# Attention matmuls in four 64x64 tiles, with background matmuls in clumps and tanhs held back, in a fused conformer block

## The chip, the cores and the metric

One core of one Trainium2 chip runs the kernel. The metric is the device time of one execution in microseconds (us), the median of several. Executions of one kernel mostly agree within 1%; a run more than 1.5% above the fastest of the same kernel is called slow and is left out of ratios.

The engines that matter: here PE does matmuls (its weight loads are listed apart, as PEld; in the changed kernel those of O start 0.02 us after matmuls of S that take 0.40 us), ACT does exp and tanh, DVE does elementwise work and copies out of PSUM. In the traces below each engine works through its instructions in program order and stands in front of one whose inputs are not ready (ACT for 0.48 us in before, in front of a tanh, with the next exp's input ready). "Granted clock" is the TensorE clock as the profile gives it: 1.0 or 0.5 in every stretch of before.

## The reference, cut to what matters

```python
B, T, D, H = 2, 4000, 144, 4                 # Dh = 36
x = x + 0.5 * (silu(layernorm(x) @ w_ff1a) @ w_ff1b)
q, k, v = heads(layernorm(x) @ w_qkv)
x = x + (softmax(q @ k.T * Dh**-0.5) @ v) @ w_o      # full attention over 4000 keys
h = layernorm(x) @ w_pw1
h = h[..., :D] * sigmoid(h[..., D:])
x = x + silu(depthwise_conv5(h)) @ w_pw2
x = x + 0.5 * (silu(layernorm(x) @ w_ff2a) @ w_ff2b)
return layernorm(x)
```

## The kernel before

Attention runs in 32 groups (batch, chunk of 500 queries, pair of heads) of 32 iterations (125 keys each), 1024 in all. One iteration is: S, scores of two heads into two PSUM banks; exp of both banks by ACT into PT; O, PT times V into one bank that accumulates over a group. A column of ones in V gives the softmax sum. Everything else (layer norms, feed-forward, convolution) is cut into small steps of Python generators, called background (bg) here. `Pump.slot` emits up to two such steps after each iteration, within a budget per engine. Sigmoid and silu are made of tanh, so bg needs ACT too.

```python
def emit_S(n):                       # two matmuls, K = 64 rows each (row tiles), M = 125
    for hh in range(2):
        op("pe", "matmul", PSV[0:TB, 2 * (n % 2) + hh, 0:CH], lhsT=KT[64 * hh:64 * hh + 64, p, k0:k0 + TB],
           rhs=QT[64 * hh:64 * hh + 64, p, q0:q0 + CH], ...)

def emit_O(n):                       # two matmuls, K = 125 rows, M = 64 (column tiles)
    for hh in range(2):
        op("pe", "matmul", PSV[64 * hh:64 * hh + 64, 4 + gi % 2, 0:CH], lhsT=VA[0:TB, blk, 2 * p + hh, :],
           rhs=PT[0:TB, n % NPT, hh, :], start=kt == 0, stop=kt == NKT - 1, ...)

def tanh_gate(bk, rows):             # emitted at once, so in front of the next exp
    t = yield from thp.take()
    op("act", "activation", TH[0:rows, t, :], PSV[0:rows, bk, 0:CH], ACT.Tanh, ...)
    return t

def epilogue(banks, b, qc, p, og):   # once per group
    op("dve", "tensor_copy", OTF[:, og % 2, :], PSV[:, 4 + og % 2, 0:CH], ...)
    yield
    bk = yield from banks.take()
    for i in range(NB):
        op("pe", "transpose", PSV[0:TB, bk, i * 128:(i + 1) * 128], OTF[:, og % 2, i * TB:(i + 1) * TB], IDF[:, :], ...)
    yield
    # ... normalise, output projection ...

emit_S(0)
for n in range(len(its)):
    if n + 1 < len(its):
        emit_S(n + 1)
    emit_exp(n)
    if n > 0:
        emit_O(n - 1)
        # ... last one of a group: pump.add(epilogue(...), first=True)
    pump.slot()                      # up to two bg steps, banks 6 and 7
```

The softmax here doesn't subtract the row's maximum and nothing guards it: scores larger than these inputs give would overflow.

Of the kernel before, what the change touches and what calls it, by code (L numbers as in the profile page):

```python
# [5 lines left out]
ACT = mybir.ActivationFunctionType  # L6
ALU = mybir.AluOpType
BF16 = mybir.dt.bfloat16
F32 = mybir.dt.float32
# [4 lines left out]
HD = 72  # L14
FF = 576
KCONV = 5
TB = 125
NB = 4
CH = 500
# [8 lines left out]
class Rec:  # L28
# [13 lines left out]
    def op(self, eng, name, *a, r=(), w=(), q=None, cost=0.0, **k):  # L42
        o = Op()
        o.eng, o.name, o.a, o.k, o.q = eng, name, a, k, q
        o.deps, o.inc, o.cnt = [], False, 0
        lane = eng if q is None else "q:" + q
        o.idx = self.n.get(lane, 0)
        self.n[lane] = o.idx + 1
        for key in r:
            h = self.hist.setdefault(key, ([], []))  # L50
            o.deps += [(d, True) for d in h[0]]
            h[1].append(o)
        for key in w:
            h = self.hist.setdefault(key, ([], []))
            o.deps += [(d, False) for d in h[0] + h[1] if d is not o]
            if h[1] and not (len(h[1]) == 1 and h[1][0] is o):
                self.hist[key] = ([o], [])
            else:
                h[0].append(o)
        self.ops.append(o)  # L60
        self.cost[eng] += cost
        return o
# [82 lines left out]
def bass_standalone__conformer_family_zipformer__speech_kernel(  # L145
# [17 lines left out]
    CPB = T // CH  # L163
    NBLK = N // TB
    NKT = T // TB

    R = Rec(nc)
    op = R.op

    def sb(name, shape, dt=BF16):  # L170
        return nc.alloc_sbuf_tensor(name, [128] + list(shape), dt)
# [9 lines left out]
    TH = sb("TH", [NTH, CH])  # L181
    HT = sb("HT", [NHT, 5, CH])
    QT = sb("QT", [2, N])
    KT = sb("KT", [2, N])
    VA = sb("VA", [NBLK, H, 64])
    NPT = 3
    PT = sb("PT", [NPT, 2, CH])
    OTF = sb("OTF", [2, CH], F32)
    RD = sb("RD", [2, NB, 2], F32)
    U = sb("U", [2, T + 4])  # L190
# [18 lines left out]
    PSV = PS[:, :].rearrange("p (b n) -> p b n", n=512)  # L209
# [138 lines left out]
            banks.give(bk)  # L348
        yield

    def tanh_gate(bk, rows):
        t = yield from thp.take()
        op("act", "activation", TH[0:rows, t, :], PSV[0:rows, bk, 0:CH], ACT.Tanh, bias=0.0, scale=0.5,
           r=[("ps", bk)], w=[("TH", t)], cost=0.47)
        return t

    def ff(banks, c, s, WA, WB, nm, silu):
        h = yield from htp.take()
# [71 lines left out]
    def post1(banks, c):  # L430
        b, cc = c // CPB, c % CPB
        s = yield from ln_tr(banks, c)
        for hf in range(2):
            bk = yield from banks.take()
            for k in range(2):
                op("pe", "matmul", PSV[0:HD, bk, 0:CH], lhsT=WP1[0:HD, k, D + hf * HD:D + (hf + 1) * HD],
                   rhs=XT[0:HD, s, k, :], start=k == 0, stop=k == 1, r=[("XT", s), "WP1"], w=[("ps", bk)], cost=0.21)
            t = yield from tanh_gate(bk, HD)
            banks.give(bk)
            bk = yield from banks.take()  # L440
            for k in range(2):
                op("pe", "matmul", PSV[0:HD, bk, 0:CH], lhsT=WP1[0:HD, k, hf * HD:(hf + 1) * HD],
                   rhs=XT[0:HD, s, k, :], start=k == 0, stop=k == 1, r=[("XT", s), "WP1"], w=[("ps", bk)], cost=0.21)
            yield
            op("dve", "scalar_tensor_tensor",
               out=U[0:HD, hf, 2 + cc * CH:2 + (cc + 1) * CH].rearrange("p (n i) -> p i n", i=NB),
               in0=TH[0:HD, t, :].rearrange("p (i n) -> p i n", i=NB), scalar=1.0,
               in1=PSV[0:HD, bk, 0:CH].rearrange("p (i n) -> p i n", i=NB), op0=ALU.add, op1=ALU.mult,
               r=[("TH", t), ("ps", bk), "U0"], w=[("U", cc)], cost=0.6)
            banks.give(bk)  # L450
            thp.give(t)
        xtp.give(s)
        yield
# [31 lines left out]

    def epilogue(banks, b, qc, p, og):
        c = b * CPB + qc
        op("dve", "tensor_copy", OTF[:, og % 2, :], PSV[:, 4 + og % 2, 0:CH], r=[("ps", 4 + og % 2)],
           w=[("OTF", og % 2)], cost=0.6)
        yield  # L490
        bk = yield from banks.take()
        for i in range(NB):
            op("pe", "transpose", PSV[0:TB, bk, i * 128:(i + 1) * 128], OTF[:, og % 2, i * TB:(i + 1) * TB],
               IDF[:, :], r=[("OTF", og % 2), "IDF"], w=[("ps", bk)], cost=0.2)
        yield
        v = PSV[0:TB, bk, :].rearrange("p (i h d) -> p i h d", i=NB, h=2)
        op("dve", "reciprocal", RD[0:TB, og % 2, :, :], v[:, :, :, DH], r=[("ps", bk)], w=[("RD", og % 2)],
           cost=0.15)
        if p == 0:
            an_slot[qc % 2] = yield from anp.take()  # L500
        a = an_slot[qc % 2]
        op("dve", "tensor_tensor",
           AN[0:TB, a, :, p * HD:(p + 1) * HD].rearrange("p i (h d) -> p i h d", h=2), v[:, :, :, 0:DH],
           RD[0:TB, og % 2, :, :].rearrange("p i (h o) -> p i h o", o=1).to_broadcast([TB, NB, 2, DH]),
           op=ALU.mult, r=[("ps", bk), ("RD", og % 2)], w=[("AN", a)], cost=0.37)
        banks.give(bk)
        yield
        if p == 1:
            s = yield from tr(banks, AN[0:TB, a, :, :], ("AN", a), lambda: anp.give(a))
            yield from residual(  # L510
                banks, c, lambda i: [(XT[0:HD, s, k, i * TB:(i + 1) * TB], WO[0:HD, k, :]) for k in range(2)], 1.0,
                [("XT", s), "WO"], 0.06)
            xtp.give(s)
            att_done.add(c)
# [37 lines left out]
    def drain(threads, width):  # L552
        live = []
        threads = list(threads)
        while threads or live:
            while threads and len(live) < width:
                live.append(threads.pop(0))
            for t in list(live):
                try:
                    next(t)  # L560
                except StopIteration:
                    live.remove(t)
# [7 lines left out]
    drain([pre(all_banks, 0, True), first()] + [pre(all_banks, c, True) for c in range(1, CPB)], 4)  # L570

    bg = Banks([6, 7])
    pump = Pump({"pe": 0.35, "dve": 0.75, "act": 0.25})

    def pre_thread(cs):
        for c in cs:
# [2 lines left out]
    def post1_thread(b):  # L579
        for c in range(b * CPB, (b + 1) * CPB):  # L580
            while c not in att_done or (b and min(c - CPB + 1, CPB - 1) not in conv_done):
                yield
            yield from post1(bg, c)
            u_done.add(c)

    def post2_thread(b):
        for c in range(b * CPB, (b + 1) * CPB):
            while c not in u_done or (c + 1 < (b + 1) * CPB and c + 1 not in u_done):
                yield
            yield from post2(bg, c)  # L590
# [4 lines left out]
    def emit_S(n):  # L595
        gi, kt = its[n]
        b, qc, p = groups[gi]
        k0 = b * T + kt * TB
        q0 = b * T + qc * CH
        kc, qcc = b * CPB + kt // NB, b * CPB + qc  # L600
        for hh in range(2):
            op("pe", "matmul", PSV[0:TB, 2 * (n % 2) + hh, 0:CH], lhsT=KT[64 * hh:64 * hh + 64, p, k0:k0 + TB],
               rhs=QT[64 * hh:64 * hh + 64, p, q0:q0 + CH], start=True, stop=True,
               r=[("WKT", kc), ("WQT", qcc)], w=[("ps", 2 * (n % 2) + hh)])

    def emit_exp(n):
        s = 2 * (n % 2)
# [3 lines left out]
    def emit_O(n):  # L611
        gi, kt = its[n]
        b, qc, p = groups[gi]
        blk = b * NKT + kt
        for hh in range(2):
            op("pe", "matmul", PSV[64 * hh:64 * hh + 64, 4 + gi % 2, 0:CH], lhsT=VA[0:TB, blk, 2 * p + hh, :],
               rhs=PT[0:TB, n % NPT, hh, :], start=kt == 0, stop=kt == NKT - 1, skip_group_check=True,
               r=[("PT", n % NPT), ("VA", blk // NB)], w=[("ps", 4 + gi % 2)])

    pump.add(pre_thread(range(CPB, NCH)))  # L620
    pump.add(post1_thread(0))
    pump.add(post2_thread(0))
    emit_S(0)
    for n in range(len(its)):
        if n + 1 < len(its):
            emit_S(n + 1)
        emit_exp(n)
        if n > 0:
            emit_O(n - 1)
            if its[n - 1][1] == NKT - 1:  # L630
                gi = its[n - 1][0]
                pump.add(epilogue(bg, *groups[gi], gi), first=True)
                if gi == CPB * 2 - 1:
                    pump.add(post1_thread(1))
                    pump.add(post2_thread(1))
        pump.slot()
    emit_O(len(its) - 1)
    gi = len(groups) - 1
    for i in (0, 1, 2, 3):
        bg.give(i)  # L640
    drain([epilogue(bg, *groups[gi], gi)] + pump.threads, 8)

    R.finish(group_qs=("w0", "w1", "w2"))
    with nc.Block() as block:
# [29 lines left out]
```

## Time and profile before

| | before |
|---|---|
| time, median of the runs at hand before the change | 1429.57 us (1429.03 to 1439.14) |
| first exp to last exp (the stage) | 1229 us |
| ahead of it / after it | 133.5 / 67 us |
| clock 0.5 within the stage | 247 us |

The page of the kernel before: busy shares in 40 slices (each digit a tenth; PEclk is the granted clock), the chain of work that ended last, and four groups of instructions (output<-inputs, shapes, count, busy us, mean ns, idle us just before and what ended it).

```profile
PE   4888899899889989888889988888888888888855
ACT  2032987787887876888976888998989898989821
PEclk9655988888998975899986999999999899989965
...
PE 51%; ACT 39%; DVE 6%; issue 1%; POOL 1%; DMA 1%; ACTq 0%; POOLq 0%; DVEq 0%
...
L121 ACT ACTIVATE PT<-PS 125x1000 bf16<-125x1000 f32 x1024 | 960.3, 1021 | 110.9 <-PE PS L121 105.2
L121 PE MATMUL PS<-QT,KT 64*125 64x500 bf16 x2048 | 469.0, 455 | 124.2 <-ACT PT L121 78.2
L121 PE MATMUL PS<-PT,VA 125*64 125x500 bf16 x2048 | 440.8, 427 | 0.6 <-ACT PT L121 0.5
...
L121 ACT ACTIVATE TH<-PS 128x500 bf16<-128x500 f32 (+1 forms) x184 | 107.9, 586 | 148.6 <-PE PS L121 148.6
```

PE and ACT share the chain, and neither is full. ACT stood idle for 148.6 us in front of tanhs that waited for PE.

One bg iteration in the timeline of before (start us, duration us, engine, instruction, count; in brackets the idle time before it and what ended it):

```profile
615.76 1.89 ACT L121 ACTIVATE PT<-PS 125x1000 bf16<-125x1000 f32 x2
...
616.81 0.42 PE L121 MATMUL PS<-QT,KT 64*125 64x500 bf16 x2 [0.72 <-ACT PT L121]
...
617.17 0.11 PEld L121 LDWEIGHTS PS<-PT,VA 125*64 125x64 bf16 x2 [0.22 <-issue]
617.17 0.40 PE L121 MATMUL PS<-PT,VA 125*64 125x500 bf16 x2
...
617.50 0.60 PE L121 MATMUL PS<-XT,WA 72*128 72x500 bf16 x2
...
618.03 0.42 PE L121 MATMUL PS<-QT,KT 64*125 64x500 bf16 x2
618.14 0.59 ACT L121 ACTIVATE TH<-PS 128x500 bf16<-128x500 f32 x1 [0.48 <-PE PS L121]
...
618.62 1.00 ACT L121 ACTIVATE PT<-PS 125x1000 bf16<-125x1000 f32 x1
```

Read it from the ACT lines. The exps end at 617.65. S for the next exp was computed at 616.81 and has been ready for long, but the tanh stands in front of that exp, and the tanh needs the WA matmuls, which PE reaches only after S and O. ACT idles 0.48 us. The steps on PE are 0.36 us (S to O) and 0.33 us (O to bg), though matmuls of 500 columns and one shape follow each other after 0.21 to 0.22 us (medians in before at full clock: 0.212 for the convolution, 0.221 for WA). Below, 0.21 us is taken for 500 columns.

For the whole stage, take the distance from each exp to the next, subtract 0.888 us (the pace of exps in a row) and 0.464 us for each tanh in between, and sum: 242 us are lost in before, 105 of them in intervals at clock 0.5.

### The profile page before, as it was taken

To read this page: it belongs to the slowest core of one execution; us is meant where nothing else is said; L and a number is where in the kernel's file an instruction comes from. 1 tells how busy PE (TensorE), PEld (TensorE's weight loads), DVE (VectorE), ACT (ScalarE), POOL (GpSimd) and SP (SyncE) were. 2 spreads that over 40 slices of the span, in tenths; PEclk is the share of its full clock that TensorE was granted. 3 is DMA by queue.
4 is the path that set the end of the run, shared out by engine and by line. 5 is a ranking of instruction groups with operands and counts; after the bars stand their busy time and mean duration, and the time that the engine had idled before them with its cause. 6 is when DMAs were issued, how large, how long until landed. Compare 5 with 4: busy or idle time off the path is not lost.

```text
span 1429.6 us, 16367 instructions
## 1 busy us (share of the span) xinstructions
PE 1225.1 (86%) x6626; PEld 492.8 (34%) x6626; DVE 527.3 (37%) x1564; ACT 1073.5 (75%) x1250; POOL 109.3 (8%) x173
## 2 busy tenths in 40 slices
PE   4888899899889989888889988888888888888855
PEld 2544333333333333332332333233333333333322
DVE  5756434344443423233332334032323232323234
ACT  2032987787887876888976888998989898989821
POOL 3120000000100000000100001000000000000001
PEclk9655988888998975899986999999999899989965
DMA  3000000000000000000000000000000000000000
GB/s 91 1 1 1 1 0 0 1 0 0 1 1 1 1 5 1 5 2 4 5 2 3 5 4 3 3 1 5 1 5 1 4 1 5 0 5 1 4 0 8
DMA packets 6397, 6.60 MB, mean 5 GB/s; under 512 B 1746, under 2 KB 6322, under 8 KB 6322
## 3 DMA queue, kind: packets, MB, share of 16 engines
q1 hardware_dynamic: 4160, 4.61, 1.0%
q10 hardware_dynamic: 2162, 0.96, 0.3%
q8 instruction: 51, 0.84, 0.2%
q14 instruction: 24, 0.20, 0.0%
HBM read 3.26 MB, written 2.30 MB: 4 GB/s over the span
## 4 chain that ended last, share of the span: by engine, by line
PE 51%; ACT 39%; DVE 6%; issue 1%; POOL 1%; DMA 1%; ACTq 0%; POOLq 0%; DVEq 0%
PE PS L121 51%; ACT PT L121 33%; ACT TH L121 6%; POOL RS L121 1%; DVE ST L121 1%; DVE XN L121 1%; DVE OTF L121 1%; DMA WB<-in_w_ff2b_dram 1%; DVE KT L121 1%; DVE XT L121 1%; DVE VA L121 0%; DVE X L121 0%; ACTq L121 0%; DVE MV L121 0%; DVE U L121 0%
## 5 line engine op out<-in xcount | busy, mean ns | idle before, releaser
L121 ACT ACTIVATE PT<-PS 125x1000 bf16<-125x1000 f32 x1024 | 960.3, 1021 | 110.9 <-PE PS L121 105.2
L121 PE MATMUL PS<-QT,KT 64*125 64x500 bf16 x2048 | 469.0, 455 | 124.2 <-ACT PT L121 78.2
L121 PE MATMUL PS<-PT,VA 125*64 125x500 bf16 x2048 | 440.8, 427 | 0.6 <-ACT PT L121 0.5
L121 PEld LDWEIGHTS PS<-QT,KT 64*125 64x125 bf16 x2048 | 141.7, 135 | 420.7 <-ACT PT L121 324.2
L121 ACT ACTIVATE TH<-PS 128x500 bf16<-128x500 f32 (+1 forms) x184 | 107.9, 586 | 148.6 <-PE PS L121 148.6
L121 PEld LDWEIGHTS PS<-PT,VA 125*64 125x64 bf16 x2048 | 114.9, 109 | 255.9 <-issue 254.7
L121 DVE SCALAR_TENSOR_TENSOR HT<-TH,PS 128x500 bf16<-128x500 bf16 x120 | 81.0, 675 | 193.5 <-ACT TH L121 193.5
L121 DVE SCALAR_TENSOR_TENSOR X<-PS,X 125x288 bf16<-125x288 f32 x128 | 58.5, 457 | 226.9 <-PE PS L121 226.7
L121 POOL TENSOR_SCALAR RS<-MV 125x4 f32<-125x4 f32 x80 | 18.4, 230 | 1308.5 <-DVE MV L121 1308.5
L121 PE MATMUL PS<-XT,WA 72*128 72x500 bf16 x320 | 115.0, 475 | 3.0 <-DVE XT L121 3.0
L121 DVE TENSOR_SCALAR XN<-X,MV,RS 125x144 bf16<-125x144 bf16 x320 | 79.4, 312 | 70.5 <-POOL RS L121 70.5
L121 POOL TENSOR_TENSOR RS<-RS,NHALF 125x4 f32<-125x4 f32 x80 | 83.4, 1043 | 6.7
L121 ACT ACTIVATE HT<-PS 128x500 bf16<-128x500 f32 x40 | 22.8, 588 | 78.8 <-PE PS L121 78.8
L121 DVE COPY XT<-PS 72x1000 bf16<-72x1000 bf16 x80 | 53.5, 676 | 75.2 <-PE PS L121 74.8
L121 PE MATMUL PS<-WB,HT 128*125 128x144 bf16 x640 | 78.9, 302 | 2.8 <-DVE HT L121 2.8
L121 PEld LDWEIGHTS PS<-WB,HT 128*125 128x125 bf16 x640 | 70.3, 201 | 23.6 <-issue 19.1
L121 DVE BATCH_NORM_STATS2 ST<-X 125x6 f32<-125x144 bf16 x320 | 77.6, 335 | 0.0
L121 PE MATMUL PS<-IDENT,XN 125*72 125x125 bf16 x512 | 49.7, 254 | 30.1 <-DVE XN L121 29.9
L121 DVE COPY OTF<-PS 128x500 f32<-128x500 f32 x32 | 21.7, 679 | 143.1 <-PE PS L121 143.1
L121 DVE SCALAR_TENSOR_TENSOR U<-TH,PS 72x500 bf16<-72x500 bf16 x32 | 40.7, 1273 | 46.8 <-PE PS L121 29.2
L121 PEld LDWEIGHTS PS<-IDENT,XN 125*72 125x72 bf16 x512 | 38.6, 135 | 46.1 <-DVE XN L121 36.1
L121 DVE SCALAR_TENSOR_TENSOR SW<-TH,PS 72x500 bf16<-72x500 bf16 x32 | 21.5, 672 | 74.2 <-ACT TH L121 74.2
(45 smaller groups left out, 469.0 us busy)
## 6 DMA issues: line engine op xcount, KB each, us to landing
X<-in_x_dram SPq DMA_DIRECT2D x16, 140.6 KB
out_dram<-XN SPq DMA_DIRECT2D x16, 140.6 KB
WA<-in_w_ff1a_dram ACTq DMA_DIRECT2D x1, 162.0 KB
WA<-in_w_ff2a_dram ACTq DMA_DIRECT2D x1, 162.0 KB
WB<-in_w_ff1b_dram ACTq DMA_DIRECT2D x1, 144.0 KB
WB<-in_w_ff2b_dram ACTq DMA_DIRECT2D x1, 144.0 KB
WQKV<-in_w_qkv_dram ACTq DMA_DIRECT2D x1, 121.5 KB
WP<-in_w_pw_dram ACTq DMA_DIRECT2D x1, 81.0 KB
```

Source lines behind the costliest of these rows:

```text
L121: ins = getattr(eng, o.name)(*o.a, **o.k)
```

## The change

The intent: S and O both become four matmuls of one tile shape (64x64), so that PE need not change shape between them. O's keys are split over the two row tiles; the two partial sums lie in banks 4 and 5 and are added on DVE at the end of a group. As those banks are no longer doubled, the first O of a group is delayed by up to three iterations (OLAG). Bg steps come in clumps of up to three after every second iteration. Tanhs that a clump asks for are held until the next exp has been emitted. DVE's write order of U changes. The diff, cut:

```diff
-    NPT = 3
+    NPT = 6
+    OLAG = 3
+    CLUMP = 2
@@ tanh_gate: put off while hold is set
+        if hold[0]:
+            held.append(emit)
+        else:
+            emit()
@@ U's write (in0 and in1 alike)
-               out=U[...].rearrange("p (n i) -> p i n", i=NB),
+               out=U[...].rearrange("p (n i) -> p n i", i=NB),
@@ epilogue
-        op("dve", "tensor_copy", OTF[:, og % 2, :], PSV[:, 4 + og % 2, 0:CH], ...)
+        op("dve", "tensor_copy", OTA[:, :], PSV[:, 4, 0:CH], ...)
+        op("dve", "tensor_tensor", OTF[:, og % 2, :], PSV[:, 5, 0:CH], OTA[:, :], op=ALU.add, ...)
@@ emit_S
-        for hh in range(2):
-            op("pe", "matmul", PSV[0:TB, 2 * (n % 2) + hh, 0:CH], lhsT=KT[64 * hh:64 * hh + 64, p, k0:k0 + TB], ...)
+        for m0, m1 in ((0, 64), (64, TB)):
+            for hh in range(2):
+                op("pe", "matmul", PSV[m0:m1, 2 * (n % 2) + hh, 0:CH],
+                   lhsT=KT[64 * hh:64 * hh + 64, p, k0 + m0:k0 + m1], ...)
@@ emit_O
-        for hh in range(2):
-            op("pe", "matmul", PSV[64 * hh:64 * hh + 64, 4 + gi % 2, 0:CH], lhsT=VA[0:TB, blk, 2 * p + hh, :], ...)
+        for r, (m0, m1) in enumerate(((0, 64), (64, TB))):
+            for hh in range(2):
+                op("pe", "matmul", PSV[64 * hh:64 * hh + 64, 4 + r, 0:CH], lhsT=VA[m0:m1, blk, 2 * p + hh, :],
+                   rhs=PT[m0:m1, n % NPT, hh, :], ...)
@@ main loop
         emit_exp(n)
-        if n > 0:
-            emit_O(n - 1)
-        pump.slot()
+        release_held()
+        emit_pending(n, 2)       # up to two O; end of a group: e = epilogue(...); next(e); pump.add(e, first=True)
+        pend.append(n)
+        if n % CLUMP == CLUMP - 1:
+            pump.slot(cap=3)     # and the budget per slot is doubled
```

More of the change, by code (lines that the diff above doesn't have):

```diff
@@ L185, in bass_standalone__conformer_family_zipformer__speech_kernel @@
     VA = sb("VA", [NBLK, H, 64])
-    NPT = 3
+    NPT = 6
+    OLAG = 3
+    CLUMP = 2
     PT = sb("PT", [NPT, 2, CH])
+    OTA = sb("OTA", [CH], F32)
     OTF = sb("OTF", [2, CH], F32)
@@ L349, in residual, with tanh_gate, emit, release_held @@
         yield
-    def tanh_gate(bk, rows):
+    held = []
+    hold = [False]
+    def tanh_gate(bk, rows, done=None):
         t = yield from thp.take()
-        op("act", "activation", TH[0:rows, t, :], PSV[0:rows, bk, 0:CH], ACT.Tanh, bias=0.0, scale=0.5,
-           r=[("ps", bk)], w=[("TH", t)], cost=0.47)
-        return t
+        def emit():
+            op("act", "activation", TH[0:rows, t, :], PSV[0:rows, bk, 0:CH], ACT.Tanh, bias=0.0, scale=0.5,
+               r=[("ps", bk)], w=[("TH", t)], cost=0.47)
+            if done:
+                done()
+        if hold[0]:
+            held.append(emit)
+        else:
+            emit()
+        return t
+    def release_held():
+        while held:
+            held.pop(0)()
     def ff(banks, c, s, WA, WB, nm, silu):
@@ L437, in post1 @@
                    rhs=XT[0:HD, s, k, :], start=k == 0, stop=k == 1, r=[("XT", s), "WP1"], w=[("ps", bk)], cost=0.21)
-            t = yield from tanh_gate(bk, HD)
-            banks.give(bk)
+            t = yield from tanh_gate(bk, HD, lambda bk=bk: banks.give(bk))
+            if hold[0]:
+                yield
             bk = yield from banks.take()
@@ L445, in post1 @@
             op("dve", "scalar_tensor_tensor",
-               out=U[0:HD, hf, 2 + cc * CH:2 + (cc + 1) * CH].rearrange("p (n i) -> p i n", i=NB),
-               in0=TH[0:HD, t, :].rearrange("p (i n) -> p i n", i=NB), scalar=1.0,
-               in1=PSV[0:HD, bk, 0:CH].rearrange("p (i n) -> p i n", i=NB), op0=ALU.add, op1=ALU.mult,
+               out=U[0:HD, hf, 2 + cc * CH:2 + (cc + 1) * CH].rearrange("p (n i) -> p n i", i=NB),
+               in0=TH[0:HD, t, :].rearrange("p (i n) -> p n i", i=NB), scalar=1.0,
+               in1=PSV[0:HD, bk, 0:CH].rearrange("p (i n) -> p n i", i=NB), op0=ALU.add, op1=ALU.mult,
                r=[("TH", t), ("ps", bk), "U0"], w=[("U", cc)], cost=0.6)
@@ L487, in epilogue @@
         c = b * CPB + qc
-        op("dve", "tensor_copy", OTF[:, og % 2, :], PSV[:, 4 + og % 2, 0:CH], r=[("ps", 4 + og % 2)],
-           w=[("OTF", og % 2)], cost=0.6)
+        op("dve", "tensor_copy", OTA[:, :], PSV[:, 4, 0:CH], r=[("ps", 4)], w=["OTA"], cost=0.65)
+        op("dve", "tensor_tensor", OTF[:, og % 2, :], PSV[:, 5, 0:CH], OTA[:, :], op=ALU.add, r=[("ps", 5), "OTA"],
+           w=[("OTF", og % 2)], cost=0.65)
         yield
@@ L572, in bass_standalone__conformer_family_zipformer__speech_kernel @@
     bg = Banks([6, 7])
-    pump = Pump({"pe": 0.35, "dve": 0.75, "act": 0.25})
+    pump = Pump({"pe": 0.35 * CLUMP, "dve": 0.75 * CLUMP, "act": 0.25 * CLUMP})
     def pre_thread(cs):
@@ L600, in emit_S @@
         kc, qcc = b * CPB + kt // NB, b * CPB + qc
-        for hh in range(2):
-            op("pe", "matmul", PSV[0:TB, 2 * (n % 2) + hh, 0:CH], lhsT=KT[64 * hh:64 * hh + 64, p, k0:k0 + TB],
-               rhs=QT[64 * hh:64 * hh + 64, p, q0:q0 + CH], start=True, stop=True,
-               r=[("WKT", kc), ("WQT", qcc)], w=[("ps", 2 * (n % 2) + hh)])
+        for m0, m1 in ((0, 64), (64, TB)):
+            for hh in range(2):
+                op("pe", "matmul", PSV[m0:m1, 2 * (n % 2) + hh, 0:CH],
+                   lhsT=KT[64 * hh:64 * hh + 64, p, k0 + m0:k0 + m1], rhs=QT[64 * hh:64 * hh + 64, p, q0:q0 + CH],
+                   start=True, stop=True, skip_group_check=True, r=[("WKT", kc), ("WQT", qcc)],
+                   w=[("ps", 2 * (n % 2) + hh)])
     def emit_exp(n):
@@ L614, in emit_O @@
         blk = b * NKT + kt
-        for hh in range(2):
-            op("pe", "matmul", PSV[64 * hh:64 * hh + 64, 4 + gi % 2, 0:CH], lhsT=VA[0:TB, blk, 2 * p + hh, :],
-               rhs=PT[0:TB, n % NPT, hh, :], start=kt == 0, stop=kt == NKT - 1, skip_group_check=True,
-               r=[("PT", n % NPT), ("VA", blk // NB)], w=[("ps", 4 + gi % 2)])
+        for r, (m0, m1) in enumerate(((0, 64), (64, TB))):
+            for hh in range(2):
+                op("pe", "matmul", PSV[64 * hh:64 * hh + 64, 4 + r, 0:CH], lhsT=VA[m0:m1, blk, 2 * p + hh, :],
+                   rhs=PT[m0:m1, n % NPT, hh, :], start=kt == 0, stop=kt == NKT - 1, skip_group_check=True,
+                   r=[("PT", n % NPT), ("VA", blk // NB)], w=[("ps", 4 + r)])
     pump.add(pre_thread(range(CPB, NCH)))
@@ L622, in bass_standalone__conformer_family_zipformer__speech_kernel, with emit_pending @@
     pump.add(post2_thread(0))
+    pend = []
+    def emit_pending(n, most):
+        for _ in range(most):
+            if not pend or pend[0] >= n or (its[pend[0]][1] == 0 and n < pend[0] + OLAG):
+                return
+            m = pend.pop(0)
+            emit_O(m)
+            gi, kt = its[m]
+            if kt == NKT - 1:
+                e = epilogue(bg, *groups[gi], gi)
+                next(e)
+                pump.add(e, first=True)
+                if gi == CPB * 2 - 1:
+                    pump.add(post1_thread(1))
+                    pump.add(post2_thread(1))
+    hold[0] = True
     emit_S(0)
@@ L627, in bass_standalone__conformer_family_zipformer__speech_kernel @@
         emit_exp(n)
-        if n > 0:
-            emit_O(n - 1)
-            if its[n - 1][1] == NKT - 1:
-                gi = its[n - 1][0]
-                pump.add(epilogue(bg, *groups[gi], gi), first=True)
-                if gi == CPB * 2 - 1:
-                    pump.add(post1_thread(1))
-                    pump.add(post2_thread(1))
-        pump.slot()
-    emit_O(len(its) - 1)
-    gi = len(groups) - 1
+        release_held()
[3 more added lines that the diff above has]
+            pump.slot(cap=3)
+    release_held()
+    hold[0] = False
+    emit_pending(len(its) + OLAG, 2 * OLAG)
     for i in (0, 1, 2, 3):
         bg.give(i)
-    drain([epilogue(bg, *groups[gi], gi)] + pump.threads, 8)
+    drain(pump.threads, 8)
     R.finish(group_qs=("w0", "w1", "w2"))
```

## The prediction

> **What bounds the kernel now.** Attention runs from the first exp (133.5 us) to the last (1363, tile view of PT); 66 us of tail follow. In the chain of waits PE has 51%, ACT 39%. The 1023 intervals between exps, sorted by what lies in them (trace, instruction by instruction):
> - no background (bg) matmul, full clock: 477 of 0.89 us, ACT's own pace;
> - bg matmul, no tanh, full clock: 257 of 1.06;
> - bg matmul and tanh, full clock: 147 of 1.99, though exp plus tanh cost ACT 0.89 + 0.48;
> - granted clock 0.5 (257 us of the stage): 142 of 1.0 to 2.8.
>
> ACT's floor is 1023 x 0.89 + 171 x 0.48 = 990 us; the stage takes 1229. Of the 240 lost, 90 lie in tanh intervals (ACT, in order, stands before a tanh whose matmul PE reaches late), 44 in other bg intervals, 105 at half clock.
>
> **Why PE is late.** The two S matmuls start within 4 ns, likewise O: pairs already run side by side. But S to O takes 0.355 us and O to the next group 0.33, where 500 columns stream in 0.21 (same-shape WA matmuls follow at 0.22). The other 0.13 us is paid at each change of shape[...]. A round S, O, bg has three: 0.36 + 0.33 + bg (0.4 to 0.55) exceeds 0.89.
>
> **The change.** S and O become four 64x64 matmuls each.[...] I expect a quad to stream in 0.21 us[...]: S+O 0.69 -> about 0.43.[...] Bg matmuls stream about 220 us in all (estimate, counts times spacings), 0.43 per clump. Two iterations on PE: 4 x 0.21 + 0.43 + 0.28 = 1.6 us, under ACT's 1.94: the stage becomes ACT bound. Held tanhs follow an exp, so the 121 us of idle before TH should nearly vanish.
>
> Added: an OTF add (32 x 0.68 us, DVE, hidden behind O's three-iteration delay); twice the PE instructions. U's write order saves 32 x 0.6 us of DVE, hidden.
>
> **What remains lost.** A clump may be about 0.5 us (1 with a tanh) before the next S is late; larger ones stall exp: estimate 0.1 us per clump, 50 us. Half clock: 20. Group starts: 10. Stage: 990 + 80 = 1070. Prologue unchanged, 133. Tail: bg threads step only every second iteration, so most of one more post2 chunk (21 us in the tail of before) is left over: 66 -> about 80.
>
> Sum 133 + 1070 + 80 = about 1280 us (-10%); range 1215 to 1350. Chances: faster 0.88, same 0.08, slower 0.04.
>
> **What would show it.** Four S starts within about 10 ns; S to O 0.21 to 0.25 us; idle of TH on PE from 121 to under 30 us; exp intervals without bg at 0.89; ACT over 65% of the chain; tail 75 to 100 us.
>
> **What would make it wrong.** Four tiles that do not run at once (quads of 0.42: PE bound again, 1400 or worse); eight weight loads per iteration that do not hide;[...] starved bg threads and a longer tail; DVE late with OTF at group starts.

The 0.28 us in the 1.6 us for two iterations is two changes of shape at 0.14 us (S to O 0.355 less 0.21). The 4 x 0.21 us supposes that four tiles stream in the time of one; at that time the traces showed it for two only, whose starts are 3 to 5 ns apart. The 0.6 us for U can be had as an estimate: it is the difference between 1.27 us for U and 0.67 for SW in the trace of before.

## More of the kernel before

From the waits within the stage (who waited for whom, us, times, longest):

```profile
ACT TH L121 <- PE PS L121: 102.6, 128, 2.0
```

## The result

| | before | after |
|---|---|---|
| time, median of 4 runs | 1433.63 us | 1250.00 us (1248.01 to 1252.64) |
| ratio, 95% interval | | 0.872 (0.868 to 0.876) |
| stage, first to last exp | 1229 us | 1041 us |
| lost in the stage, as above | 242 us | 57 us |
| ahead of it / after it | 133.5 / 67 us | 133.6 / 73 us |
| clock 0.5 within the stage | 247 us | 35 us |

A ratio is the mean time of one kernel's fast runs over that of the other's of the same rounds, so not quite the ratio of the medians. All runs of the experiments gave a correct result.

The same lines of the page of the changed kernel:

```profile
PE   3888787878888888888877788887877777878754
ACT  2221799999999998999999998999999999999711
PEclk9756799999999998999999988999999999999855
...
ACT 63%; PE 24%; DVE 9%; POOL 1%; issue 1%; DMA 1%; ACTq 0%; POOLq 0%; DVEq 0%
...
L121 ACT ACTIVATE PT<-PS 125x1000 bf16<-125x1000 f32 x1024 | 949.4, 1059 | 51.0 <-PE PS L121 49.6
L121 PE MATMUL PS<-QT,KT 64*64 64x500 bf16 (+1 forms) x4096 | 412.3, 398 | 151.6 <-ACT PT L121 141.4
L121 PE MATMUL PS<-PT,VA 61*64 61x500 bf16 (+1 forms) x4096 | 385.4, 377 | 0.5 <-ACT PT L121 0.4
...
L121 ACT ACTIVATE TH<-PS 128x500 bf16<-128x500 f32 (+1 forms) x184 | 115.9, 637 | 58.6 <-PE PS L121 57.6
```

ACT is now full in the stage, the clock stays up, and the idle time before tanhs fell from 148.6 to 57.6 us; within the stage it fell from 103 to 8 us. From the waits within the stage, as above:

```profile
PEld PS L121 <- ACT PT L121: 497.6, 770, 1.6
...
PEld PS L121 <- DVE OTF L121: 36.5, 28, 1.8
PE PS L121 <- DVE OTF L121: 27.9, 28, 1.3
...
ACT TH L121 <- PE PS L121: 8.4, 14, 2.4
```

PE now waits for ACT. The waits for OTF, the sum of the two parts of O, have grown: matmuls stand for it 28 times, 27.9 us in all, where in before one matmul did, for 0.8 us. The timeline of the changed kernel, quads alone and then with a bg clump:

```profile
599.56 7.31 ACT L121 ACTIVATE PT<-PS 125x1000 bf16<-125x1000 f32 x8
...
602.44 0.11 PEld L121 LDWEIGHTS PS<-QT,KT 64*64 64x64 bf16 x4 [0.75 <-ACT PT L121]
602.45 0.40 PE L121 MATMUL PS<-QT,KT 64*64 64x500 bf16 x4 [0.28 <-ACT PT L121]
602.47 0.11 PEld L121 LDWEIGHTS PS<-PT,VA 64*64 64x64 bf16 x4
602.68 0.38 PE L121 MATMUL PS<-PT,VA 64*64 64x500 bf16 x4
...
603.34 0.41 PE L121 MATMUL PS<-QT,KT 64*64 64x500 bf16 x4 [0.28 <-ACT PT L121]
...
603.58 0.38 PE L121 MATMUL PS<-PT,VA 64*64 64x500 bf16 x4
...
603.89 0.46 PE L121 MATMUL PS<-WO,XT 72*125 72x144 bf16 x4
```

S to O takes 0.235 us (median at full clock), where the pairs took 0.355. The four matmuls of S start within 10 ns (median; 14 at most) and their four weight loads are done in 0.11 us together. The weights of O load 0.02 us after S has started, while S still streams (602.47); in before they were loaded 0.36 us after it, when S was nearly through, and O's matmuls started with them (both at 617.17 above). So the tile mode does on PE just what was foreseen. Whether it is what made the kernel faster is a question for experiments.

The other half of the change, a held tanh, in the same trace:

```profile
431.55 4.58 ACT L121 ACTIVATE PT<-PS 125x1000 bf16<-125x1000 f32 x5
...
435.41 0.59 PE L121 MATMUL PS<-XT,WA 72*128 72x500 bf16 x2
...
436.04 0.59 ACT L121 ACTIVATE TH<-PS 128x500 bf16<-128x500 f32 x1
...
436.52 1.89 ACT L121 ACTIVATE PT<-PS 125x1000 bf16<-125x1000 f32 x2
```

The WA matmuls end at 436.00 while an exp still runs, and the tanh follows that exp without idle time.

### The profile page after: what moved, and what is told of

Read it like the earlier page. It is cut to its first block, busy times and chain, and to the rows that moved or that the text cites. A ratio compares the mean times of both kernels' runs of the same rounds, so it can differ in the third digit from the quotient of the medians.

```text
span 1247.4 us, 24613 instructions
## 1 busy us (share of the span) xinstructions
PE 987.3 (79%) x10722; PEld 377.0 (30%) x10722; DVE 535.6 (43%) x1596; ACT 1041.1 (83%) x1250; POOL 109.2 (9%) x173
## 3 DMA queue, kind: packets, MB, share of 16 engines
q8 instruction: 84, 1.38, 0.5%
## 4 chain that ended last, share of the span: by engine, by line
ACT 63%; PE 24%; DVE 9%; POOL 1%; issue 1%; DMA 1%; ACTq 0%; POOLq 0%; DVEq 0%
ACT PT L121 58%; PE PS L121 24%; ACT TH L121 5%; DVE OTF L121 2%; DVE OTA L121 2%; POOL RS L121 1%; DVE ST L121 1%; DVE XN L121 1%; DMA WB<-in_w_ff2b_dram 1%; DVE KT L121 1%; DVE VA L121 0%; DVE X L121 0%; ACTq L121 0%; DVE XT L121 0%; DVE MV L121 0%
## 5 line engine op out<-in xcount | busy, mean ns | idle before, releaser
L121 ACT ACTIVATE PT<-PS 125x1000 bf16<-125x1000 f32 x1024 | 949.4, 1059 | 51.0 <-PE PS L121 49.6
L121 PE MATMUL PS<-QT,KT 64*64 64x500 bf16 (+1 forms) x4096 | 412.3, 398 | 151.6 <-ACT PT L121 141.4
L121 PE MATMUL PS<-PT,VA 61*64 61x500 bf16 (+1 forms) x4096 | 385.4, 377 | 0.5 <-ACT PT L121 0.4
L121 PEld LDWEIGHTS PS<-QT,KT 64*64 64x64 bf16 (+1 forms) x4096 | 113.8, 104 | 532.3 <-ACT PT L121 495.5
L121 ACT ACTIVATE TH<-PS 128x500 bf16<-128x500 f32 (+1 forms) x184 | 115.9, 637 | 58.6 <-PE PS L121 57.6
L121 PEld LDWEIGHTS PS<-PT,VA 61*64 61x64 bf16 (+1 forms) x4096 | 119.9, 108 | 18.0 <-issue 4.7
L121 PE MATMUL PS<-WB,HT 128*125 128x144 bf16 x640 | 60.3, 255 | 5.4 <-DVE HT L121 3.6
L121 PEld LDWEIGHTS PS<-WB,HT 128*125 128x125 bf16 x640 | 54.6, 161 | 21.7 <-issue 8.7
L121 DVE SCALAR_TENSOR_TENSOR U<-TH,PS 72x500 bf16<-72x500 bf16 x32 | 32.3, 1009 | 43.3 <-ACT PT L121 27.0
L121 DVE COPY OTA<-PS 128x500 f32<-128x500 f32 x32 | 21.7, 679 | 64.7 <-PE PS L121 64.7
L121 PE MATMUL PS<-IDF,OTF 128*125 128x128 f32 x128 | 23.4, 307 | 29.4 <-DVE OTF L121 29.4
```

The source lines that it names most:

```text
L121: ins = getattr(eng, o.name)(*o.a, **o.k)
```

## The experiments

My theory at this point was that of the prediction: PE was late because each change of tile shape costs about 0.12 us (S to O 0.355 us in before, 0.235 in the changed kernel), and the tiles cured it. The rival: the new schedule (held tanhs, clumps) cured it. Ratios below are against runs of before on the same chip.

### pairs_in_clumps: the new schedule, the old tile shapes

```diff
 (the changed kernel, with emit_S, emit_O and the copy of OTF as in before: two matmuls each, O in bank 4 + gi % 2)
```

> The new schedule (clumps, held tanhs, U's write order) with S and O as pairs in their old tile shapes. Theory[...]: PE needs about 2 x 0.69 + 0.43 + 0.13 = 1.94 us for two iterations, just ACT's 1.94, so stalls stay and half clock too: about 1340 us (1310 to 1380), S to O still 0.355 us. Rival (the schedule, above all the held tanhs, gives most of the gain): under 1290 us. Idle of TH on PE should fall to under 70 us by either.

The theory is the one just told, with the prediction's 0.13 us for a change of shape; that is also the 0.13 in the sum, which stays at 1.94 us.

Measured: 1259.0 us, ratio 0.876 (0.872 to 0.880). S to O is still 0.355 us. The theory said 1340, the rival under 1290: the rival holds. The profiled run was a slow one (1277 us), so its losses (86 us) are not compared.

### quads_old_schedule: the new tile shapes, the old schedule

```diff
-    CLUMP = 2
+    CLUMP = 1
-    hold[0] = True
-            pump.slot(cap=3)
+            pump.slot()
```

> Quads with the old schedule: one slot of two steps after every iteration, tanh emitted at once. Theory (both parts count): a tanh still stands in front of an exp and waits for its matmul, about 0.45 us in each of some 150 such intervals, so about 1320 us (1290 to 1350), with idle of TH on PE of 70 us or more in the stage; S to O 0.24 us. Rival (the tiles alone give it): 1250 to 1265 us, idle of TH on PE as in the changed kernel (58 us).

Measured: 1430.1 us, ratio 0.996 (0.992 to 1.000), no gain at all. S to O is 0.235 us, so PE does save its time; 242 us are lost in the stage, just as in before. ACT idles 142.8 us before tanhs. Both expectations missed. From its timeline, a tanh in front of an exp:

```profile
615.82 0.81 PEld L121 LDWEIGHTS PS<-U,DG 72*72 72x72 bf16 x5
615.88 1.22 PE L121 MATMUL PS<-U,DG 72*72 72x500 bf16 x5
...
617.13 0.58 ACT L121 ACTIVATE TH<-PS 72x500 bf16<-72x500 f32 x1 [1.43 <-PE PS L121]
...
617.62 2.77 ACT L121 ACTIVATE PT<-PS 125x1000 bf16<-125x1000 f32 x3
```

The quads don't help here: the tanh waits for the five convolution matmuls, and the exp, whose S is ready, waits behind the tanh. But the sum over intervals showed a second thing. The second interval of each group was 1.90 us too long, 61 us in all:

```profile
285.10 0.68 DVE L121 COPY OTA<-PS 128x500 f32<-128x500 f32 x1 [1.03 <-PE PS L121]
285.88 0.68 DVE L121 TENSOR_TENSOR OTF<-PS,OTA 128x500 f32<-128x500 f32 x1
286.62 0.70 PE L121 MATMUL PS<-IDF,OTF 128*125 128x128 f32 x4 [1.55 <-DVE OTF L121]
...
287.71 1.90 ACT L121 ACTIVATE PT<-PS 125x1000 bf16<-125x1000 f32 x2 [1.80 <-PE PS L121]
```

The changed kernel emits the copies at the end of a group at once, and a slot after every iteration then puts the transposes of OTF right behind them. PE stands in front of the transposes for the two DVE operations, 1.55 us, and the next S stands behind. This run is therefore the tiles plus a stall of my own making; quads_old_late below mends it.

### quad_s_pair_o: is the cost of a change of shape real, and does it matter?

```diff
 (the changed kernel, with emit_O and the copy of OTF as in before)
```

> New schedule, S as quads, O as the old pairs, so the tile shape changes between S and O again. Theory[...]: S to O goes back to about 0.35 us although S is four tiles, and the time is that of pairs_in_clumps within 2%. Rival (smaller tiles are faster in themselves, each quad giving half): midway between pairs_in_clumps and the changed kernel, about 1295 us, S to O under 0.30 us.

Measured: 1247.5 us, ratio 0.870 (0.866 to 0.873); S to O is 0.335 us. So the cost of a change of shape is real: the same four-tile S is followed by O after 0.335 us when O has another shape and after 0.235 when it has the same. The difference is 0.10 us. In this run O's weights load only with O's matmuls, 0.33 us after S, not 0.02 us after it as in the changed kernel; whether the cost lies in the change of shape itself or in that later load was not separated:

```profile
603.43 0.41 PE L121 MATMUL PS<-QT,KT 64*64 64x500 bf16 x4
...
603.76 0.11 PEld L121 LDWEIGHTS PS<-PT,VA 125*64 125x64 bf16 x2 [0.22 <-issue]
```

Whether it matters, the time does not decide. The expected time (that of pairs_in_clumps within 2%) came out, but pairs_in_clumps, this run and the changed kernel lie within 1% of each other (0.876, 0.870, 0.872). And this run differs from the changed kernel in more than the shape of O: it has no add for OTF, and the third interval of its groups is 0.37 us too long, in the changed kernel 0.98 (12 and 31 us in all). Without the third intervals it loses 44 us and the changed kernel 25. So the changes of shape may cost some 20 us here (an estimate, 44 less 25), hidden by the stall that the add brings with it; no run separates the two.

### hold_only and clumps_only: which part of the schedule?

The new theory: ACT's order. In the traces ACT did not pass over a tanh that had to wait: it idled 0.48 us (before) and 1.43 us (quads_old_schedule) with the next exp's input ready. Both runs use pairs.

```diff
 hold_only (from pairs_in_clumps)              clumps_only (from pairs_in_clumps)
-    CLUMP = 2                                 -        if hold[0]:
+    CLUMP = 1                                 -            held.append(emit)
-            pump.slot(cap=3)                  -        else:
+            pump.slot()                       -            emit()
                                               +        emit()
```

> Pairs (old tile shapes), slots of two steps after every iteration as before, but tanhs held until after the next exp. My first theory has fallen: tiles with the old schedule gave 1430 us, the new schedule with pairs 1259. New theory (ACT's order: a tanh in front of an exp waits for a matmul that PE reaches late; held, it waits for nothing): most of the gain is here, 1270 to 1320 us, idle of TH on PE under 75 us (121 in the stage of before and 57 outside it). Rival (the clumps, fewer changes of shape and fewer late S, give the gain): 1370 us or more.

> Pairs, clumps of up to three steps every second iteration, tanhs emitted at once, so in front of the next exp. Theory (ACT's order): the wait of a tanh for its matmul stays, behind a longer clump, so 1360 to 1440 us, with idle of TH on PE of 140 us or more. Rival (clumps): under 1320 us.

Measured: hold_only 1345.9 us, ratio 0.936 (0.932 to 0.940), less than expected; ACT idles 73.5 us before tanhs (in its profiled run, a slow one), as expected. Clumps_only 1539.8 us, four runs from 1517 to 1565 with no ratio given, as three of them count as slow; even the fastest is 5% above any run of before. Clumps by themselves are harmful: ACT idles 227.7 us before tanhs, and 629 us of the 1357 us stage of the profiled run (a slow one) are at clock 0.5. From its timeline:

```profile
801.98 1.02 PE L121 MATMUL PS<-XT,WA 72*128 72x500 bf16 x2
802.93 0.68 PE L121 MATMUL PS<-QT,KT 64*125 64x500 bf16 x2
803.04 0.59 ACT L121 ACTIVATE TH<-PS 128x500 bf16<-128x500 f32 x1 [1.38 <-PE PS L121]
```

In this stretch at half clock the two WA matmuls take 1.02 us (0.60 in the stretch of before) and the pair of S 0.68 (0.42), and the tanh waits 1.38 us in place of 0.48.

### hold_late, quads_old_late: the same without the stall at group starts

In hold_only (profiled in a slow run) the second interval of each group was again too long, by 1.24 us. Both runs give the epilogue two yields more, so that the transposes come two slots later.

```diff
            w=[("OTF", og % 2)], ...)
         yield
+        yield
+        yield
         bk = yield from banks.take()
```

> As quads_old_schedule (1430 us), with the transposes of the epilogue two slots later. There the second interval of each group was 1.9 us too long, 61 us in all, because PE stood in front of transposes of an OTF that the extra add delivers later. Theory (the tiles' gain was eaten by that stall): 1370 us, between 1355 and 1390. Rival (the tiles gain nothing even so, what PE saves is waited for elsewhere): over 1410 us.

> As hold_only (pairs, tanhs held, a slot after every iteration; 1346 us), with the transposes of the epilogue two slots later. In hold_only the second interval of each group was 1.24 us too long (40 us in all). Theory (that stall hid a part of what the held tanhs give): 1300 to 1320 us, and what is still missing to the clumps' 1259 is the bg rounds on PE, three changes of tile shape in each, 1.24 us against 0.89. Rival (nothing more to gain by holding): over 1335 us.

Measured: quads_old_late 1355.5 us, ratio 0.945 (0.941 to 0.949), at the edge of what was expected: the tiles without held tanhs and clumps do gain 5.5%, and with the stall there was nothing left of it. (The loss fell by 79 us, more than the 61 of the stall: the time at clock 0.5 fell too, from 274 us to 157.) Hold_late 1291.1 us, ratio 0.900 (0.897 to 0.903), more than expected: held tanhs without tiles and clumps gain 10%. ACT's waits before tanhs in hold_late, whole run (148.6 us, 144 times in before):

```profile
ACT TH L121 <- PE PS L121: 58.1, 55, 13.3
```

### quads_hold_late: both, without clumps

```diff
 (quads_old_late with hold[0] = True: tanhs held)
```

> Quads, tanhs held, transposes two slots later, a slot of two steps after every iteration: all but the clumps. Theory (tiles and clumps are two cures for the same thing, too little room on PE in one iteration with bg work, so with tiles and held tanhs the clumps are hardly needed): 1240 to 1285 us. Rival (clumps are needed with either tile shape): 1300 us or more.

Measured: 1243.4 us, ratio 0.868 (0.866 to 0.869); 55 us lost in the stage. That is all that the changed kernel gains, without the clumps. With pairs the clumps do gain: 1291 (hold_late) to 1259 us (pairs_in_clumps).

### late_transposes and mixed_late: can the waits for OTF be had back?

```diff
 (one more yield at the same place: late_transposes in the changed kernel, mixed_late in quad_s_pair_o)
```

> The changed kernel with one more yield in the epilogue, so that the four fp32 transposes of OTF come one slot (two iterations) later. In the trace of the changed kernel the third interval of each group is 0.98 us longer than it need be, 32 of them, 31 of the 57 us that the stage loses, and PE waits for DVE OTF 29 times. Theory (PE stands in order in front of those transposes): these waits vanish and the time falls by 25 to 31 us, to about 1222 us (ratio to before 0.852). Rival (it is the first O of the next group, or S, that waits for DVE): under 8 us faster, and the excess stays at the start of the group.

> As quad_s_pair_o (1247.5 us; S as quads, O as pairs in two banks by turns, clumps, held tanhs), with the transposes one slot later; a candidate for the best. Its third interval of each group was 0.37 us too long, 12 us in all. Theory (PE stands in front of the transposes): 1236 to 1240 us. Rival (other work of the clump takes the time anyway): 1246 to 1249 us.

Measured: late_transposes 1241.8 us, ratio 0.865 (0.863 to 0.868), about 8 us faster than the changed kernel where 25 to 31 were expected. The waits of PE for OTF did vanish (from 29 to 1), and the third interval of a group is 0.40 us too long instead of 0.98; but the fifth went from 0.11 to 0.47, and one group shows what took the place of the wait:

```profile
291.02 0.68 DVE L121 COPY OTA<-PS 128x500 f32<-128x500 f32 x1 [2.22 <-PE PS L121]
291.80 0.68 DVE L121 TENSOR_TENSOR OTF<-PS,OTA 128x500 f32<-128x500 f32 x1
292.40 0.67 DVE L121 CAST KT<-PS 128x500 bf16<-128x500 f32 x1
292.98 0.99 DVE L121 SCALAR_TENSOR_TENSOR U<-TH,PS 72x500 bf16<-72x500 bf16 x1
293.12 0.60 PE L121 MATMUL PS<-XT,WK 72*128 72x500 bf16 x2 [1.75 <-DVE KT L121]
```

The copies to OTA and OTF stand in DVE's queue in front of the copies that set bg's only two banks free. The next bg matmul in the clump needs such a bank, and PE waits 1.75 us for KT instead of for OTF. The wait was moved in part, not removed. Mixed_late was a miss: 1257.7 us, ratio 0.880 (0.877 to 0.882), slower than quad_s_pair_o (0.870). Its third interval fell from 0.37 to 0.22 us too long, its fifth rose from 0.09 to 0.46. These two make 7 of the 12 us that its stage loses more than that of quad_s_pair_o; why was not followed further.

### warm_before: what the low clock costs by itself

In before, every stretch at one clock within the stage lasts a whole multiple of 3.41 us. Counting streamed columns (500 in 0.21 us, an fp32 transpose of 128 at its 0.109) in windows of that length, the 19 windows at full clock that were followed by clock 0.5 had a median streamed share of 0.38, those that were not, 0.56. In before, S and O alone at ACT's pace reach 0.47 on average (two times 0.21 us in 0.89), and alone they were seldom followed by clock 0.5: 47 stretches of nothing else on PE for over 4 us (first to last start of a matmul), one of them 28 us long, kept full clock to their end. It fell after 3.8 and 4.0 us in two others, both with a pause of 0.88 us on PE behind a tanh. In 16 of the 19 windows a tanh started.

```diff
         if n + 1 < len(its):
+            if quiet:            # the last slot gave PE no bg work
+                emit_dup(n + 1)  # S(n + 1) for the first 256 queries, overwritten by the full S
             emit_S(n + 1)
```

> The kernel before, with 256 columns of the next S computed twice (same tile shape, same banks, same values) in iterations whose last slot gave PE nothing else. In before, [...]105 us of the 242 that the stage loses lie at clock 0.5. Theory (a low share of streaming in the stretches of S and O alone drops the clock, and that costs about 100 us): less than 100 us of the stage at clock 0.5, and 1340 to 1400 us. Rival (the low clock only goes along with stalls that would cost the same): time within 1% of before or slower, though the clock is up.

The theory's cause, a low share in stretches of S and O alone, was a guess: by the count above 47 of 49 such stretches kept full clock. What the run tests is whether more streamed columns go with less time at clock 0.5, and what that is worth.

Measured: 1411.7 us, ratio 0.983 (0.979 to 0.987). Time at clock 0.5 in the stage fell from 247 to 100 us and the loss in it from 105 to 47 us; but the loss at full clock rose from 137 to 174, as the extra columns delay PE where bg work follows. The gain is between what theory and rival expected. What is shown: with more columns streamed, this run spent 147 us less of the stage at clock 0.5, and 58 us of loss at that clock went with it. That the whole 105 could be had this way is not shown.

### old_u: the write order of U

```diff
-               out=U[...].rearrange("p (n i) -> p n i", i=NB),   (in0 and in1 alike)
+               out=U[...].rearrange("p (n i) -> p i n", i=NB),
```

> The changed kernel with U's old write order. DVE then takes 1.27 us for each of 32 instead of 1.01 us, 8 us more of DVE, whose share is under half. Theory (off the chain): the time stays within 0.4% of the changed kernel, 1245 to 1255 us. Rival (DVE in order, so a late U makes a later HT, OTA or X late, on which PE waits): 1256 us or more.

Measured: 1252.2 us, ratio 0.874 (0.871 to 0.876), the same as the changed kernel. DVE takes 1.27 us per U with this order (trace of before) and 1.01 with the other (changed kernel); it is off the chain.

### The parts side by side

| S and O | tanh | slots | transposes | run | median us | ratio |
|---|---|---|---|---|---|---|
| pairs | at once | each | as before | before | 1433 | 1 |
| quads | at once | each | early | quads_old_schedule | 1430 | 0.996 |
| quads | at once | each | late | quads_old_late | 1355 | 0.945 |
| pairs | held | each | early | hold_only | 1346 | 0.936 |
| pairs | held | each | late | hold_late | 1291 | 0.900 |
| pairs | at once | clumps | early | clumps_only | 1540 | none |
| pairs | held | clumps | early | pairs_in_clumps | 1259 | 0.876 |
| quads | held | clumps | early | after | 1250 | 0.872 |
| quads | held | clumps | late | late_transposes | 1242 | 0.865 |
| quads | held | each | late | quads_hold_late | 1243 | 0.868 |

All but the first also carry the small edits (OLAG, six PT buffers, U, the copies at the end of a group at once), which were not run by themselves, except for U; nor were later transposes with pairs and tanhs at once. So the gains of quads_old_late and hold_late over before hold what those edits are worth. Free of that are two comparisons on top of each other's part: the tiles, quads_hold_late against hold_late, 0.868 / 0.900 = 0.964; and the held tanhs, quads_hold_late against quads_old_late, 0.868 / 0.945 = 0.918 (each against its own runs of before). Late_transposes and quads_hold_late both beat the changed kernel by about 0.6%: their runs lie between 1240.3 and 1244.0 us, those of the changed kernel between 1248.0 and 1252.6, though not in the same rounds. Quads_hold_late needs no clumps and is the simpler one.

## Why the prediction was right or wrong

The number was right: 1250 us against 1280 (1215 to 1350). The reason given for it was only a part of the truth, and the number could not tell: held tanhs with pairs in clumps (1259 us), with tiles in place of clumps (1243) and with both (1250) all end within 1.3% of each other. Luck had a part too: the errors of the terms, below, went both ways.

**Held.** ACT's floor (990 us, 984 by the sum above) and the stage that becomes ACT bound: 1041 us, 57 of them lost. S to O 0.235 us, four starts within 10 ns (median): four 64x64 tiles ran side by side here, as two tiles did in before (3 to 5 ns). Exps without bg at 0.89 us. Idle of tanhs on PE within the stage from 103 to 8 us (the prediction's 121 was counted up to 1390 us, beyond the last exp).

**Failed: "Why PE is late", and from it "the stage becomes ACT bound" because two iterations take PE 1.6 us.** This step counts how much work PE has and asks whether it is under ACT's 1.94. By that sum pairs in clumps need 2 x 0.69 + 0.43 + 0.13 = 1.94 us, and I expected 1340 us of them; they ran in 1259. The quads saved PE 0.12 us in each iteration and with the old schedule and the changed kernel's epilogue gained nothing. What made ACT idle was less the sum on PE than the order on ACT: a tanh that is emitted in front of an exp makes ACT wait for the last item of PE's round, whatever is in it. Held tanhs wait behind an exp of 0.89 us, and PE is done by then (in the changed kernel ACT idles 8 us before tanhs in the whole stage). The prediction had this mechanism, in one sentence, as a consequence; it is the largest single part (10.0% over before, 8.2% on top of the tiles). Much of this lay at half clock: from before to hold_late the loss fell from 137 to 78 us in intervals at full clock and from 105 to 22 in those at half clock; to quads_old_late, from 137 to 112 and from 105 to 51.

**Not additive.** Held tanhs gain 10.0% and tiles 5.5% over before, each without the other. If they were independent the ratio of both would be 0.900 x 0.945 = 0.851; it is 0.868, as both fill the same idle time of ACT, and 55 us above the floor is what is left. When held tanhs and clumps are there, the tiles as built gain about 0.5% (0.872 against 0.876, with intervals that overlap). In part that is the stall of their add: the third intervals lose 31 us in the changed kernel and 13 in pairs_in_clumps (a slow run). The clumps gain nothing when held tanhs and tiles are there (0.865 against 0.868).

**Sizes.** Clumps were to cost 50 us: 18 us are lost at full clock outside the group starts. Half clock was to cost 20: 7. Group starts were to cost 10: 31, all of it in the third interval of a group, where PE stands in front of the transposes of OTF. "DVE, hidden behind O's three-iteration delay" was wrong in this: O was delayed, the transposes were not. The tail was to grow to 80 us because a chunk of bg work is left over: 73. ACT's share of the chain is 63%, not over 65.

**Open.** The stage was at clock 0.5 for 247 us in before, for 35 in the changed kernel, and for 100 in warm_before, which streams more columns. How much of the gain of the held tanhs goes through the clock, and why clumps by themselves are as bad as 1540 us, was not separated; that waits bring the low clock about was not shown by a run.

## What to carry to other kernels

When two engines take turns and neither is full, look at the order in the queue of the one that idles before making the other faster: an instruction that needs a late result belongs behind one whose input is ready. An engine saved by tiling gives time only where it is the one waited for, and a change that adds a step to a result (here an add on two halves) must move the readers of that result back as well. Run each half of a compound change by itself; here a right number hid that the tiles, as built and with the other half in place, were worth about half a per cent, and 3.6% with their stall mended and no clumps.

## What this case measured of the hardware

- S to O took 0.355 us from 64x125 to 125x64 pairs (before), 0.335 from 64x64 quads to 125x64 pairs (quad_s_pair_o), and 0.235 with 64x64 for both (the changed kernel).
- With quads the weight loads of O, which go to the same two halves of the rows (0 to 63 and 64 up) that S is using, started 0.02 us after S's matmuls, and O followed S after 0.235 us, about the 0.21 us that 500 columns take. They are hidden. With O as pairs they started with O's matmuls, 0.36 us after S in before and 0.33 in quad_s_pair_o.
- In the stage of before the clock went to 0.5 after windows of 3.41 us with a median streamed share of 0.38; windows at full clock that kept it had a median of 0.56. The share alone does not tell the two apart: 11 of the 12 windows under 0.40 were followed by clock 0.5, 4 of the 11 from 0.40 to 0.435, and the other 4 had 0.44 to 0.54; in the changed kernel one of the two windows under 0.40 (both 0.38) kept full clock. Full clock came back in before after 20 windows that streamed 0.76 to 0.85 of what half clock can (500 columns in 0.42 us, twice the 0.21; WP's matmuls follow each other after 0.424 at clock 0.5); after 52 others, with 0.61 to 0.77, it did not.
- The same 72x500 bf16 operation on DVE took 1.27 us writing with a step of four elements (U in before), 1.01 writing in order and reading with long steps (U in the changed kernel), and 0.67 writing in order and reading with a step of four (SW in both). The prediction had put the saving for U at 0.6 us; it was 0.26.
